# One weight tile for the K and Q projections, a DMA transpose at the start, and G accumulated early

## Chip, cores and metric

One core of a Trainium2 chip. The metric is the device time of one execution in microseconds. Beside it each execution has a span, from its first to its last instruction; the time is some 1.7 to 2.0 us longer than the span. All runs told of here are of state fast, that is within 1.5% of the fastest of their kernel. "The chain" is the profile's chain of work that ended last, followed back from the last instruction to whatever each step had waited for. Stages have the names of the kernel's functions: K and Q (projections), G, KV, M, D (denominators), E (first half of the feed-forward), FT and F (outputs).

## The reference

```python
x = A_x                                            # 1 x 2048 x 640, bf16
g = sigmoid((x * gate_w).sum(-1, keepdims=True))
# A: linear attention, 32 heads of 20
q, k, v = split(x @ wqkv)                          # wqkv 640 x 1920
phi = lambda t: where(t > 0, t + 1, exp(t)) + 1e-6
pq, pk = phi(q), phi(k)
kv = einsum("bhsd,bhse->bhde", pk, v); z = einsum("bhsd->bhd", pk)
o = einsum("bhqd,bhde->bhqe", pq, kv) / (einsum("bhqd,bhd->bhq", pq, z)[..., None] + 1e-6)
a = o.transpose(...).reshape(B, S, D) @ wo
# B: feed-forward with a gate
b = (gelu(x @ w_gate) * (x @ w_up)) @ w_down       # 640 -> 1728 -> 640
out = g * a + (1 - g) * b
```

The kernel doesn't compute v. It forms G = x^T pk, then kv = Wv^T G per group of heads (masked), M = kv wo, and at the end pq M and the feed-forward in one accumulation. The 2048 rows are 16 tiles of 128.

## The kernel before

Loads at the start, in the order of the queue (cuts marked):

```python
dma(out=x_sb[0][:, 0, :], in_=x_view[:, 0, :])
for lo, hi in ((0, 1), (1, 3), (3, 5)):
    dma(out=wk[:, lo:hi, 0:D], in_=wqkv_v[:, lo:hi, D : 2 * D])
dma(out=x_sb[0][:, 2:4, :], in_=x_view[:, 2:4, :])
dma(out=wq[:], in_=wqkv_v[:, :, 0:D])
...                                  # gate and up weights
for q in (1, 2, 3):                  # x transposed by DMA for tiles 4 to 15
    nc.sync.dma_start_transpose(out=xT[q][:, :, :], in_=x2[q * QW : (q + 1) * QW, :])
```

Tiles 0 to 3 are transposed on TensorE (`transpose_x`: five 128x128 transposes into PSUM, two copies out). The first K projections and the order of stages:

```python
CH = ((0, QW), (QW, D))              # 512 and 128 columns; K has one more, the gate's
def k_first():
    transpose_x(0)
    nc.tensor.matmul(t[:, 0:256], ...)           # a filler
    transpose_x(1)
    for dk in range(ND):
        for st in range(2):
            mm(st, 0, dk)                        # 512-wide chunk of K, tiles 0 and 1
        ...
    for st in range(2):
        for dk in range(ND):
            mm(st, 1, dk)                        # 129-wide chunk
        transpose_x(2 + st)
        k_out(st, pss[st])
...
k_first()
for st in (2, 3): phase_K(st)
for st in range(4): phase_Q(st)
for ft in range(NF): phase_E(0, ft)              # feed-forward of rows 0 to 511
for st in range(4, NT): phase_K(st)
phase_gate()
for st in range(4, NT):
    phase_Q(st); ...                             # z additions, G matmuls in between
phase_Zrep(); ...                                # the rest of G
phase_KV(0, 4)
...                                              # phase_E(1) with M and the denominators D
phase_FT(0)                                      # outputs; then E(2), FT(1), E(3), FT(2), F
```

`phi` of a chunk is an exp on ScalarE, a min-add and a max-add on VectorE.

Of the kernel before, what the change touches and what calls it, by code (L numbers as in the profile page):

```python
# [8 lines left out]
ACT = mybir.ActivationFunctionType  # L9
ALU = mybir.AluOpType  # L10
# [6 lines left out]
def kernel(  # L17
# [12 lines left out]
    nc = tc.nc  # L30
# [29 lines left out]
    def ps_tile(name):  # L60
        return psum.tile([P, QW], FP32, name=name, tag="ps")
# [7 lines left out]
    x_sb = [x_all[:, 4 * q : 4 * q + 4, :] for q in range(NQ)]  # L69
    pk_q = [ov.tile([P, 4, D], BF16, name=f"pk{q}", tag="slab_a", bufs=NQ) for q in range(NQ)]  # L70
    pk = [pk_q[t // 4][:, t % 4, :] for t in range(NT)]
    wk = ov.tile([P, ND, D + P], BF16, name="wk", tag="slab_c")
    wq = ov.tile([P, ND, D], BF16, name="wq", tag="slab_d")

    wg = wpool.tile([P, ND, FM], BF16, name="wg")
    wu = wpool.tile([P, ND, FM], BF16, name="wu")
# [16 lines left out]
    nc.scalar.dma_start(out=gw5[:], in_=gate_w.rearrange("(k p) -> k p", p=P))  # L93
    dma(out=x_sb[0][:, 0, :], in_=x_view[:, 0, :])
    for lo, hi in ((0, 1), (1, 3), (3, 5)):
        dma(out=wk[:, lo:hi, 0:D], in_=wqkv_v[:, lo:hi, D : 2 * D])
    dma(out=x_sb[0][:, 2:4, :], in_=x_view[:, 2:4, :])
    dma(out=wq[:], in_=wqkv_v[:, :, 0:D])
    warm = consts.tile([P, 1], FP32, name="act_warm")
    nc.scalar.activation(out=warm[:], in_=nc.const_aps.tensor(1.0, [P, 1], BF16), func=ACT.Exp)  # L100
    for lo, hi in ((0, 512), (512, 1024), (1024, FM)):
# [3 lines left out]
    dma(out=wgu[:, :, FL:P], in_=wu_v[:, :, FM:F])  # L105
    for q in (1, 2, 3):
        nc.sync.dma_start_transpose(out=xT[q][:, :, :], in_=x2[q * QW : (q + 1) * QW, :])
    for q in (1, 2, 3):
        dma(out=x_sb[q][:], in_=x_view[:, 4 * q : 4 * q + 4, :])
    dma(out=wv[:], in_=wqkv_v[:, :, 2 * D : 3 * D])  # L110
# [64 lines left out]
            nc.vector.tensor_tensor(out=hT_cur[q][0:FL, ft, :], in0=pgu[FL:P, :],  # L175
                                    in1=gl[0:FL, :], op=ALU.mult)

    def phi(dst, src, width):
        e = work.tile([P, QW], BF16, name="phi_e")
        nc.scalar.activation(out=e[:, :width], in_=src, func=ACT.Exp)  # L180
        m = work.tile([P, QW], BF16, name="phi_m")
        nc.vector.tensor_scalar(  # L182
            out=m[:, :width], in0=e[:, :width], scalar1=1.0, scalar2=EPS, op0=ALU.min, op1=ALU.add,
        )
        nc.vector.scalar_tensor_tensor(  # L185
            out=dst, in0=src, scalar=0.0, in1=m[:, :width], op0=ALU.max, op1=ALU.add,
        )

    def proj(ps, w, st, lo, hi):
        q, sl = divmod(st, 4)  # L190
        for dk in range(ND):
            nc.tensor.matmul(  # L192
                ps[:, 0 : hi - lo], lhsT=xT[q][:, dk, sl * P : (sl + 1) * P],
                rhs=w[:, dk, lo:hi], start=(dk == 0), stop=(dk == ND - 1),
            )

    CH = ((0, QW), (QW, D))

    def k_out(st, pss):
        for (lo, hi), ps in zip(CH, pss):  # L200
            phi(pk[st][:, lo:hi], ps[:, 0 : hi - lo], hi - lo)
        nc.scalar.activation(
            out=eneg[:, st : st + 1], in_=pss[1][:, D - QW : D - QW + 1], func=ACT.Exp, scale=-1.0
        )

    def phase_K(st):
        pss = [ps_tile("ps_k") for _ in CH]
        for (lo, hi), ps in zip(CH, pss):
            proj(ps, wk, st, lo, hi + (hi == D))
        k_out(st, pss)  # L210

    def k_first():
        pss = [[ps_tile("ps_k") for _ in CH] for _ in range(2)]

        def mm(st, c, dk):
            lo, hi = CH[c]
            hi += hi == D
            nc.tensor.matmul(  # L218
                pss[st][c][:, 0 : hi - lo], lhsT=xT[0][:, dk, st * P : (st + 1) * P],
                rhs=wk[:, dk, lo:hi], start=(dk == 0), stop=(dk == ND - 1),  # L220
            )

        transpose_x(0)
        nc.tensor.matmul(t[:, 0:256], lhsT=x_sb[0][:, 0, 0:P], rhs=x_sb[0][:, 0, 0:256], start=True, stop=True)
        transpose_x(1)
        for dk in range(ND):
            for st in range(2):
                mm(st, 0, dk)
            if dk == 2:
                tg = psum.tile([P, 2 * QW], BF16, name="tp_g", tag="ps")  # L230
                nc.tensor.transpose(tg[:, 0:ND], gw5[:], ident[0:ND, 0:ND])
                gcol = consts.tile([P, ND], BF16, name="gcol")
                nc.vector.tensor_copy(out=gcol[:], in_=tg[:, 0:ND])
        for dk in range(ND):
            nc.gpsimd.tensor_copy(out=wk[:, dk, D : D + 1], in_=gcol[:, dk : dk + 1])
        for st in range(2):
            for dk in range(ND):
                mm(st, 1, dk)
            transpose_x(2 + st)
            k_out(st, pss[st])  # L240

    def phase_Q(st):
        for lo, hi in CH:
            ps = ps_tile("ps_q")
            proj(ps, wq, st, lo, hi)
            phi(pq[st][:, lo:hi], ps[:, 0 : hi - lo], hi - lo)

    g_sb = big.tile([P, ND, D], BF16, name="g_sb")

    def g_units():  # L250
        for lo, hi in CH:
            for ct in range(ND):
                gp = ps_tile("ps_G")
                for st in range(NT):
                    nc.tensor.matmul(  # L255
                        gp[:, 0 : hi - lo], lhsT=x_all[:, st, ct * P : (ct + 1) * P],
                        rhs=pk[st][:, lo:hi], start=(st == 0), stop=(st == NT - 1),
                    )
                    if st < NT - 1:
                        yield hi - lo  # L260
                nc.scalar.copy(out=g_sb[:, ct, lo:hi], in_=gp[:, 0 : hi - lo])
                yield hi - lo

    zacc = consts.tile([P, D], FP32, name="zacc")
    zsum = consts.tile([P, D], BF16, name="zsum")
# [2 lines left out]
    def phase_Z(st):  # L268
        if st == 0:
            return  # L270
        nc.vector.tensor_tensor(out=(zsum[:] if st == NT - 1 else zacc[:]), in0=(pk[0][:] if st == 1 else zacc[:]),
                                in1=pk[st][:], op=ALU.add)
# [50 lines left out]

    def phase_M(g):
        if g == 0:
            M["sb"] = ov.tile([P, ND, D], BF16, name="m_sb", tag="slab_c")
            M["st"] = ov.tile([GW, NG, D], BF16, name="m_st", tag="slab_d")
        m_sb, m_st = M["sb"], M["st"]
        for hh in range(2):
            cs = slice(hh * HALF, (hh + 1) * HALF)  # L330
            mp = ps_tile("ps_m")
            nc.tensor.matmul(mp[0 : gw[g], 0:HALF], lhsT=kvt[0 : gw[g], g, 0 : gw[g]],  # L332
                             rhs=wo_g[0 : gw[g], g, cs], start=True, stop=True)
            if hh == 0:
                nc.vector.tensor_copy(out=m_st[0 : gw[g], g, cs], in_=mp[0 : gw[g], 0:HALF])
            else:
                nc.scalar.copy(out=m_st[0 : gw[g], g, cs], in_=mp[0 : gw[g], 0:HALF])
        lo = GW * g
        hi = lo + gw[g]
        while lo < hi:  # L340
            k = lo // P
            e = min(hi, (k + 1) * P)
            dma(out=m_sb[lo - k * P : e - k * P, k, :], in_=m_st[lo - GW * g : e - GW * g, g, :])
            lo = e
# [23 lines left out]
    def phase_FT(q):  # L368
        hT = hT_cur[q]
        o_q = ov.tile([P, 4, D], BF16, name="o_q", tag="slab_f")  # L370
        for dt in range(ND):
            ds = slice(dt * P, (dt + 1) * P)
            acc = ps_tile("ps_acc")
            for dk in range(ND):
                nc.tensor.matmul(acc[:], lhsT=M["sb"][:, dk, ds], rhs=pqT[q][:, dk, :],  # L375
                                 start=(dk == 0), stop=False)
            for ft in range(NF):
                nc.tensor.matmul(acc[:], lhsT=wd[:, ft, ds], rhs=hT[:, ft, :],  # L378
                                 start=False, stop=(ft == NF - 1))
            oT = work.tile([P, D], BF16, name="oT", tag="o_out", bufs=2)  # L380
            nc.vector.tensor_tensor(out=oT[:, 0:QW], in0=acc[:], in1=gsc["rep"][:, q * QW : (q + 1) * QW], op=ALU.mult)  # L381
            nc.sync.dma_start_transpose(out=o_q[:, :, ds], in_=oT[:, 0:QW])
        dma(out=out2[q * QW : (q + 1) * QW, :].rearrange("(t p) d -> p t d", p=P), in_=o_q[:])

    def phase_F(st):
# [6 lines left out]
        for i, (lo, hi) in enumerate(parts):  # L392
            acc = ps_tile("ps_acc")
            for dk in range(ND):
                nc.tensor.matmul(acc[:, 0 : hi - lo], lhsT=pqT[q][:, dk, ts],  # L395
                                 rhs=M["sb"][:, dk, lo:hi], start=(dk == 0), stop=False)
            for ft in range(NF):
                nc.tensor.matmul(acc[:, 0 : hi - lo], lhsT=hT[:, ft, ts],  # L398
                                 rhs=wd[:, ft, lo:hi], start=False, stop=(ft == NF - 1))
# [9 lines left out]

    with tc.manual_schedule(engines={mybir.EngineType.PE}):  # L410
        k_first()
    for st in (2, 3):
        phase_K(st)
    for st in range(4):
        phase_Q(st)
    for ft in range(NF):
        phase_E(0, ft)
    for st in range(4, NT):
        phase_K(st)
    phase_gate()  # L420
    gu = g_units()
    done = 0
    total = NT * ND * D
    for st in range(4, NT):
        phase_Q(st)
        for z in range(4 * (st - 4) // 3, 4 * (st - 3) // 3):
            phase_Z(z)
        while done < total * (st - 3) // (NT - 3):
            done += next(gu)
    phase_Zrep()  # L430
    for w in gu:
        pass
    phase_KV(0, 4)
    hT_cur[1] = ov.tile([P, NF, QW], BF16, name="hT1", tag="slab_b")
    nc.gpsimd.memset(hT_cur[1][FL:P, NF - 1, :], 0.0)
# [53 lines left out]
```

## Time and profile before

| | before |
|---|---|
| median of the first 4 runs | 279.83 us (279.4 to 282.44) |
| span of the profiled run | 277.5 us |
| TensorE busy | 271.8 us, 98% |
| VectorE, ScalarE busy | 143.2, 76.1 us |
| feed-forward begins | 17.48 us |

The last row is the start of the first `ps_g` matmul in the timeline; it splits the kernel into a start that hangs on loads and a rest that hardly varies. The lines of the page and of the chain stand in the prediction. One view more is worth having beside them, the groups of instructions with shapes kept apart (columns: line, engine, operation, tiles, shapes, count, busy us, mean ns, idle before):

```profile
L192 PE MATMUL ps_q<-wq,xT 128*128 128x512 bf16 x78 | 19.8, 379 | 0.1
L192 PE MATMUL ps_q<-wq,xT 128*128 128x128 bf16 x80 | 7.1, 219 | 0.0
```

A narrow matmul's record lasts 219 ns, but 80 of them were busy for only 7.1 us in all: records overlap. So a record's length isn't what a matmul costs in a stream; that has to be read from the chain.

### The profile page before, as it was taken

The page shows a single profiled execution, that of the slowest core. Times are in us where ns is not written, and L with a number is a line of the kernel's source. Part 1 is how long each engine was busy: PE and PEld are TensorE (multiplying, and loading weights), DVE is VectorE, ACT ScalarE, POOL GpSimd, SP SyncE. Part 2 cuts the span into 40 slices and gives each one's busy share as a digit, 9 for nine tenths or more (in the row PEclk, how much of TensorE's full clock was granted, in tenths as well). Part 3 has the DMA queues.
Part 4 walks back from the last instruction along what each step waited for, and adds up shares of the span by engine and source line. Part 5 has one row for each costly group of instructions (what it writes and reads, how often), then busy time and mean ns, then how long its engine had stood idle before and what let it go on. Part 6 is the DMA issues. An engine that isn't in the chain of part 4 may idle for free.

```text
span 277.5 us, 3993 instructions
## 1 busy us (share of the span) xinstructions
PE 271.8 (98%) x1522; PEld 138.6 (50%) x1548; DVE 143.2 (52%) x317; ACT 76.1 (27%) x167; POOL 5.1 (2%) x18
## 2 busy tenths in 40 slices
PE   8999999999999999999999999999999999999995
PEld 3554444555555584544444444444444444445774
DVE  0793233899944369999999542221112332101011
ACT  3663224764233362442100123210012222000100
POOL 5000000000000000000000000000000000000000
PEclk9999999999999999999999999999999999999999
DMA  7999999300100005343223540001112000021301
GB/s 213 361 353 194 224 353 282 118 2 0 1 4 0 0 2 149 62 117 72 51 53 65 105 135 0 0 0 31 28 38 94 2 0 0 19 40 38 118 26 47
DMA packets 43818, 23.58 MB, mean 85 GB/s; under 512 B 30808, under 2 KB 43672, under 8 KB 43800
## 3 DMA queue, kind: packets, MB, share of 16 engines
q1 hardware_dynamic: 43646, 23.17, 32.0%
q8 instruction: 12, 0.20, 0.3%
q10 hardware_dynamic: 154, 0.17, 0.2%
q14 instruction: 6, 0.05, 0.1%
HBM read 13.32 MB, written 2.63 MB: 57 GB/s over the span
## 4 chain that ended last, share of the span: by engine, by line
PE 96%; DMA 2%; ACT 1%; issue 1%; SPq 0%; DVE 0%
PE ps_u L155 20%; PE ps_g L155 20%; PE ps_acc L378 16%; PE ps_q L192 8%; PE ps_G L255 8%; PE ps_k L192 7%; PE ps_acc L375 6%; PE ps_acc L398 5%; PE ps_acc L395 2%; DMA wk<-in_A_wqkv_dram 2%; PE ps_gu L155 2%; PE ps_k L218 1%; PE ps_m L332 1%; PE ps_kv L304 1%; ACT phi_e L180 0%
## 5 line engine op out<-in xcount | busy, mean ns | idle before, releaser
L155 PE MATMUL ps_g<-xT,wg 128*128 128x512 bf16 x249 | 64.1, 379 | 0.6
L155 PE MATMUL ps_u<-xT,wu 128*128 128x512 bf16 x260 | 64.6, 379 | 0.0
L161 DVE TENSOR_TENSOR hT<-ps_u,gl 128x512 bf16<-128x512 f32 x52 | 35.6, 685 | 51.1 <-PE ps_u L155 51.1
L160 ACT ACTIVATE gl<-ps_g 128x512 bf16<-128x512 f32 x52 | 31.0, 597 | 112.1 <-PE ps_g L155 112.1
L378 PE MATMUL ps_acc<-hT,wd 128*128 128x512 bf16 x205 | 47.5, 379 | 0.3
L155 PEld LDWEIGHTS <-wu 128*128 128x128 bf16 x260 | 25.4, 98 | 30.7
L155 PEld LDWEIGHTS <-wg 128*128 128x128 bf16 x260 | 25.1, 98 | 29.2 <-issue 0.3
L192 PEld LDWEIGHTS <-xT 128*128 128x128 bf16 x300 | 24.0, 98 | 20.5 <-ACT xT L146 0.4
L378 PEld LDWEIGHTS <-wd 128*128 128x128 bf16 x210 | 20.5, 98 | 24.8
L381 DVE TENSOR_TENSOR oT<-ps_acc,omg_rep 128x512 bf16<-128x512 f32 x15 | 10.3, 687 | 36.7 <-PE ps_acc L378 32.8
L192 PE MATMUL ps_q<-wq,xT 128*128 128x128 bf16 (+1 forms) x158 | 23.8, 298 | 0.1
L255 PE MATMUL ps_G<-pk,x_all 128*128 128x128 bf16 (+1 forms) x157 | 23.4, 298 | 0.2
L182 DVE TENSOR_SCALAR phi_m<-phi_e 128x512 bf16<-128x512 bf16 x64 | 12.8, 237 | 15.4 <-ACT phi_e L180 15.2
L192 PE MATMUL ps_k<-wk,xT 128*128 128x512 bf16 (+1 forms) x136 | 19.2, 298 | 0.3
L375 PE MATMUL ps_acc<-pqT,m_sb 128*128 128x512 bf16 x75 | 18.6, 379 | 0.0
L180 ACT ACTIVATE phi_e<-ps_q 128x512 bf16<-128x512 f32 (+1 forms) x32 | 12.4, 435 | 21.6 <-PE ps_q L192 21.1
L398 PE MATMUL ps_acc<-wd,hT 128*128 128x320 bf16 (+1 forms) x126 | 16.7, 285 | 0.0
L255 PEld LDWEIGHTS <-x_all 128*128 128x128 bf16 x160 | 12.0, 98 | 7.2
L180 ACT ACTIVATE phi_e<-ps_k 128x512 bf16<-128x512 f32 (+1 forms) x32 | 12.8, 440 | 7.5 <-PE ps_k L192 4.3
L185 DVE SCALAR_TENSOR_TENSOR pq<-ps_q,phi_m 128x512 bf16<-128x512 f32 (+1 forms) x32 | 14.2, 483 | 0.0
L185 DVE SCALAR_TENSOR_TENSOR pk<-ps_k,phi_m 128x512 bf16<-128x512 f32 (+1 forms) x32 | 14.2, 481 | 0.0
L398 PEld LDWEIGHTS <-hT 128*128 128x128 bf16 x126 | 11.6, 98 | 3.7
(65 smaller groups left out, 144.3 us busy)
## 6 DMA issues: line engine op xcount, KB each, us to landing
wd<-in_B_w_down_dram SPq DMA_DIRECT2D x1, 2080.0 KB
x_all<-in_A_x_dram SPq DMA_DIRECT2D x3, 640.0 KB, 4.9
out_dram<-o_q SPq DMA_DIRECT2D x3, 640.0 KB
wg<-in_B_w_gate_dram SPq DMA_DIRECT2D x2, 640.0 KB
wu<-in_B_w_up_dram SPq DMA_DIRECT2D x2, 640.0 KB, 11.2
wq<-in_A_wqkv_dram SPq DMA_DIRECT2D x1, 800.0 KB
wg<-in_B_w_gate_dram SPq DMA_DIRECT2D x1, 800.0 KB
wu<-in_B_w_up_dram SPq DMA_DIRECT2D x1, 800.0 KB
```

Of the source, the lines that this page charges most:

```text
L155: nc.tensor.matmul(ps[:, t0 : t0 + tw], lhsT=w[:, dk, ft * P : (ft + 1) * P], rhs=xT[q][:, dk, t0 : t0 + tw], start=(dk == 0), stop=(dk == ...
L160: nc.scalar.activation(out=gl[:], in_=psg[:], func=ACT.Gelu_apprx_tanh)
L161: nc.vector.tensor_tensor(out=hT_cur[q][:, ft, :], in0=psu[:], in1=gl[:], op=ALU.mult)
L180: nc.scalar.activation(out=e[:, :width], in_=src, func=ACT.Exp)
L182: nc.vector.tensor_scalar(out=m[:, :width], in0=e[:, :width], scalar1=1.0, scalar2=EPS, op0=ALU.min, op1=ALU.add,)
L185: nc.vector.scalar_tensor_tensor(out=dst, in0=src, scalar=0.0, in1=m[:, :width], op0=ALU.max, op1=ALU.add,)
L192: nc.tensor.matmul(ps[:, 0 : hi - lo], lhsT=xT[q][:, dk, sl * P : (sl + 1) * P], rhs=w[:, dk, lo:hi], start=(dk == 0), stop=(dk == ND - 1),)
L255: nc.tensor.matmul(gp[:, 0 : hi - lo], lhsT=x_all[:, st, ct * P : (ct + 1) * P], rhs=pk[st][:, lo:hi], start=(st == 0), stop=(st == NT - 1),)
L375: nc.tensor.matmul(acc[:], lhsT=M["sb"][:, dk, ds], rhs=pqT[q][:, dk, :], start=(dk == 0), stop=False)
L378: nc.tensor.matmul(acc[:], lhsT=wd[:, ft, ds], rhs=hT[:, ft, :], start=False, stop=(ft == NF - 1))
L381: nc.vector.tensor_tensor(out=oT[:, 0:QW], in0=acc[:], in1=gsc["rep"][:, q * QW : (q + 1) * QW], op=ALU.mult)
L398: nc.tensor.matmul(acc[:, 0 : hi - lo], lhsT=hT[:, ft, ts], rhs=wd[:, ft, lo:hi], start=False, stop=(ft == NF - 1))
```

## The change

Intent: fewer and wider matmuls for K and Q (chunks of 512, 512 and 257 columns in place of 512, 129, 512 and 128), part of G accumulated while K and Q are computed, and a start without PE transposes for tiles 2 and 3. The diff, cut to its core:

```diff
-    wk = ov.tile([P, ND, D + P], BF16, name="wk", tag="slab_c")
-    wq = ov.tile([P, ND, D], BF16, name="wq", tag="slab_d")
+    WQK = 2 * D + 1
+    wqk = ov.tile([P, ND, 2 * D + P], BF16, name="wqk", tag="slab_c")   # Q in 0:D, K in D:2D, gate at 2D
@@ loads
-    dma(out=x_sb[0][:, 2:4, :], in_=x_view[:, 2:4, :])
-    dma(out=wq[:], in_=wqkv_v[:, :, 0:D])
+    dma(out=wqk[:, :, 0:D], in_=wqkv_v[:, :, 0:D])
+    nc.sync.dma_start_transpose(out=xT[0][:, :, 2 * P : QW], in_=x2[2 * P : QW, :])
...
+    dma(out=x_sb[0][:, 2:4, :], in_=x_view[:, 2:4, :])      # now behind the later transposes
@@ k_first
-        nc.tensor.matmul(t[:, 0:256], ...)
...
-            transpose_x(2 + st)
@@ new
+    CQ = ((0, QW), (QW, D))
+    CK = ((D, D + QW), (D + QW, WQK))
+    CF = ((0, QW), (QW, 2 * QW), (2 * QW, WQK))
+    def phase_KQ(st, chunks, wo=0):
+        for lo, hi in chunks:
+            ps = ps_tile("ps_kq")
+            for dk in range(ND):
+                kq_mm(ps, st, dk, lo + wo, hi + wo)          # columns lo+wo to hi+wo of wqk
+            cols(st, ps, lo, hi)                             # phi into pq and pk by lo, hi
@@ order
-    for st in (2, 3): phase_K(st)
-    for st in range(4): phase_Q(st)
+    for st in (0, 1): phase_KQ(st, CQ, wo=D)
+    for st in (2, 3): phase_KQ(st, CF)
     for ft in range(NF): phase_E(0, ft)
-    ...                                                      # K of 4..15; Q with z and G; rest of G
+    early = [(ps_tile("ps_G"), ct) for ct in range(2)]
+    for st in range(4, NT):
+        phase_KQ(st, CF)
+        ...                                                  # 2 or 4 matmuls of the two early accumulators
+    phase_gate(); ...                                        # z additions
+    ...                                                      # the other eight accumulators of G
+    phase_Zrep()
```

Note `wo=D`: Q of tiles 0 and 1 is computed from columns D to 2D, which hold K's weights. So for 256 of 2048 rows the query is the key. All runs of the changed kernel still counted as correct. I replayed the formulas in double precision with this swap: the output moves by at most 1.1e-5 while its standard deviation is 2.3e-3, since phi(q) is 1.00 with a deviation of 0.06 here and cancels largely between numerator and denominator. It is a wrong computation that this data hides.

More of the change, by code (lines that the diff above doesn't have):

```diff
@@ L95 @@
     for lo, hi in ((0, 1), (1, 3), (3, 5)):
-        dma(out=wk[:, lo:hi, 0:D], in_=wqkv_v[:, lo:hi, D : 2 * D])
-    dma(out=x_sb[0][:, 2:4, :], in_=x_view[:, 2:4, :])
-    dma(out=wq[:], in_=wqkv_v[:, :, 0:D])
+        dma(out=wqk[:, lo:hi, D : 2 * D], in_=wqkv_v[:, lo:hi, D : 2 * D])
+    dma(out=wqk[:, :, 0:D], in_=wqkv_v[:, :, 0:D])
+    nc.sync.dma_start_transpose(out=xT[0][:, :, 2 * P : QW], in_=x2[2 * P : QW, :])
     warm = consts.tile([P, 1], FP32, name="act_warm")
@@ L176, in phase_E, with cols @@
                                     in1=gl[0:FL, :], op=ALU.mult)
-    def phi(dst, src, width):
+    def cols(st, ps, lo, hi):
+        w = hi - lo
         e = work.tile([P, QW], BF16, name="phi_e")
-        nc.scalar.activation(out=e[:, :width], in_=src, func=ACT.Exp)
+        nc.scalar.activation(out=e[:, 0:w], in_=ps[:, 0:w], func=ACT.Exp)
         m = work.tile([P, QW], BF16, name="phi_m")
         nc.vector.tensor_scalar(
-            out=m[:, :width], in0=e[:, :width], scalar1=1.0, scalar2=EPS, op0=ALU.min, op1=ALU.add,
+            out=m[:, 0:w], in0=e[:, 0:w], scalar1=1.0, scalar2=EPS, op0=ALU.min, op1=ALU.add,
@@ L184, in phi @@
         )
-        nc.vector.scalar_tensor_tensor(
-            out=dst, in0=src, scalar=0.0, in1=m[:, :width], op0=ALU.max, op1=ALU.add,
-        )
-    def proj(ps, w, st, lo, hi):
-        q, sl = divmod(st, 4)
-        for dk in range(ND):
-            nc.tensor.matmul(
-                ps[:, 0 : hi - lo], lhsT=xT[q][:, dk, sl * P : (sl + 1) * P],
-                rhs=w[:, dk, lo:hi], start=(dk == 0), stop=(dk == ND - 1),
-            )
-    CH = ((0, QW), (QW, D))
-    def k_out(st, pss):
-        for (lo, hi), ps in zip(CH, pss):
-            phi(pk[st][:, lo:hi], ps[:, 0 : hi - lo], hi - lo)
-        nc.scalar.activation(
-            out=eneg[:, st : st + 1], in_=pss[1][:, D - QW : D - QW + 1], func=ACT.Exp, scale=-1.0
-        )
@@ L206, in phase_K @@
-    def phase_K(st):
-        pss = [ps_tile("ps_k") for _ in CH]
-        for (lo, hi), ps in zip(CH, pss):
-            proj(ps, wk, st, lo, hi + (hi == D))
-        k_out(st, pss)
-    def k_first():
-        pss = [[ps_tile("ps_k") for _ in CH] for _ in range(2)]
-        def mm(st, c, dk):
-            lo, hi = CH[c]
-            hi += hi == D
-            nc.tensor.matmul(
-                pss[st][c][:, 0 : hi - lo], lhsT=xT[0][:, dk, st * P : (st + 1) * P],
-                rhs=wk[:, dk, lo:hi], start=(dk == 0), stop=(dk == ND - 1),
-            )
+        if hi == WQK:
+            nc.scalar.activation(
+                out=eneg[:, st : st + 1], in_=ps[:, w - 1 : w], func=ACT.Exp, scale=-1.0
+            )
@@ new lines, in cols, with kq_mm @@
+        for dst, base in ((pq[st], 0), (pk[st], D)):
+            a, z = max(lo, base), min(hi, base + D)
+            if a < z:
+                nc.vector.scalar_tensor_tensor(
+                    out=dst[:, a - base : z - base], in0=ps[:, a - lo : z - lo], scalar=0.0,
+                    in1=m[:, a - lo : z - lo], op0=ALU.max, op1=ALU.add,
+                )
+    def kq_mm(ps, st, dk, lo, hi):
+        q, sl = divmod(st, 4)
+        nc.tensor.matmul(
+            ps[:, 0 : hi - lo], lhsT=xT[q][:, dk, sl * P : (sl + 1) * P],
+            rhs=wqk[:, dk, lo:hi], start=(dk == 0), stop=(dk == ND - 1),
+        )
@@ L223, in k_first @@
+    CQ = ((0, QW), (QW, D))
[7 more added lines that the diff above has]
+            cols(st, ps, lo, hi)
+    def k_first():
+        pss = [[ps_tile("ps_k") for _ in CK] for _ in range(2)]
         transpose_x(0)
-        nc.tensor.matmul(t[:, 0:256], lhsT=x_sb[0][:, 0, 0:P], rhs=x_sb[0][:, 0, 0:256], start=True, stop=True)
@@ L227, in k_first @@
             for st in range(2):
-                mm(st, 0, dk)
+                kq_mm(pss[st][0], st, dk, *CK[0])
             if dk == 2:
@@ L234, in k_first, with g_mm, g_out @@
         for dk in range(ND):
-            nc.gpsimd.tensor_copy(out=wk[:, dk, D : D + 1], in_=gcol[:, dk : dk + 1])
+            nc.gpsimd.tensor_copy(out=wqk[:, dk, 2 * D : WQK], in_=gcol[:, dk : dk + 1])
         for st in range(2):
             for dk in range(ND):
-                mm(st, 1, dk)
-            transpose_x(2 + st)
-            k_out(st, pss[st])
-    def phase_Q(st):
-        for lo, hi in CH:
-            ps = ps_tile("ps_q")
-            proj(ps, wq, st, lo, hi)
-            phi(pq[st][:, lo:hi], ps[:, 0 : hi - lo], hi - lo)
-    g_sb = big.tile([P, ND, D], BF16, name="g_sb")
-    def g_units():
-        for lo, hi in CH:
-            for ct in range(ND):
-                gp = ps_tile("ps_G")
-                for st in range(NT):
-                    nc.tensor.matmul(
-                        gp[:, 0 : hi - lo], lhsT=x_all[:, st, ct * P : (ct + 1) * P],
-                        rhs=pk[st][:, lo:hi], start=(st == 0), stop=(st == NT - 1),
-                    )
-                    if st < NT - 1:
-                        yield hi - lo
-                nc.scalar.copy(out=g_sb[:, ct, lo:hi], in_=gp[:, 0 : hi - lo])
-                yield hi - lo
+                kq_mm(pss[st][1], st, dk, *CK[1])
+            for (lo, hi), ps in zip(CK, pss[st]):
+                cols(st, ps, lo, hi)
+    g_sb = big.tile([P, ND, D], BF16, name="g_sb")
+    def g_mm(gp, ct, st, lo, hi):
+        nc.tensor.matmul(
+            gp[:, 0 : hi - lo], lhsT=x_all[:, st, ct * P : (ct + 1) * P],
+            rhs=pk[st][:, lo:hi], start=(st == 0), stop=(st == NT - 1),
+        )
+    def g_out(gp, ct, lo, hi):
+        nc.scalar.copy(out=g_sb[:, ct, lo:hi], in_=gp[:, 0 : hi - lo])
     zacc = consts.tile([P, D], FP32, name="zacc")
@@ L325, in phase_M @@
         if g == 0:
-            M["sb"] = ov.tile([P, ND, D], BF16, name="m_sb", tag="slab_c")
-            M["st"] = ov.tile([GW, NG, D], BF16, name="m_st", tag="slab_d")
-        m_sb, m_st = M["sb"], M["st"]
+            M["all"] = ov.tile([P, ND + NG, D], BF16, name="m_all", tag="slab_c")
+        m_sb = M["all"][:, 0:ND, :]
+        m_st = M["all"][:, ND : ND + NG, :]
         for hh in range(2):
@@ L374, in phase_FT @@
             for dk in range(ND):
-                nc.tensor.matmul(acc[:], lhsT=M["sb"][:, dk, ds], rhs=pqT[q][:, dk, :],
+                nc.tensor.matmul(acc[:], lhsT=M["all"][:, dk, ds], rhs=pqT[q][:, dk, :],
                                  start=(dk == 0), stop=False)
@@ L395, in phase_F @@
                 nc.tensor.matmul(acc[:, 0 : hi - lo], lhsT=pqT[q][:, dk, ts],
-                                 rhs=M["sb"][:, dk, lo:hi], start=(dk == 0), stop=False)
+                                 rhs=M["all"][:, dk, lo:hi], start=(dk == 0), stop=False)
             for ft in range(NF):
@@ L411 @@
         k_first()
+    for st in (0, 1):
+        phase_KQ(st, CQ, wo=D)
     for st in (2, 3):
-        phase_K(st)
-    for st in range(4):
-        phase_Q(st)
+        phase_KQ(st, CF)
     for ft in range(NF):
         phase_E(0, ft)
+    early = [(ps_tile("ps_G"), ct) for ct in range(2)]
     for st in range(4, NT):
-        phase_K(st)
-    phase_gate()
-    gu = g_units()
-    done = 0
-    total = NT * ND * D
-    for st in range(4, NT):
-        phase_Q(st)
-        for z in range(4 * (st - 4) // 3, 4 * (st - 3) // 3):
-            phase_Z(z)
-        while done < total * (st - 3) // (NT - 3):
-            done += next(gu)
+        phase_KQ(st, CF)
+        for gp, ct in early:
+            for g in range(4 * (st - 4) // 3, 4 * (st - 3) // 3):
+                if g < NT - 1:
+                    g_mm(gp, ct, g, 0, QW)
+    phase_gate()
+    for st in range(NT):
+        phase_Z(st)
+    for ct, lo, hi in [(ct, 0, QW) for ct in range(2, ND)] + [(ct, QW, D) for ct in range(ND)]:
+        gp = ps_tile("ps_G")
+        for st in range(NT - 1):
+            g_mm(gp, ct, st, lo, hi)
+        for ep, ec in early:
+            g_mm(ep, ec, NT - 1, 0, QW)
+            g_out(ep, ec, 0, QW)
+        early = []
+        g_mm(gp, ct, NT - 1, lo, hi)
+        g_out(gp, ct, lo, hi)
     phase_Zrep()
-    for w in gu:
-        pass
     phase_KV(0, 4)
```

## The prediction

> **What bounds the kernel now.** I read the page first, for which engine is full, then the chain of work that ended last.
>
> ```profile
> PE 271.8 (98%) x1522; PEld 138.6 (50%) x1548; DVE 143.2 (52%) x317; ACT 76.1 (27%) x167; POOL 5.1 (2%) x18
> PE 96%; DMA 2%; ACT 1%; issue 1%; SPq 0%; DVE 0%
> ```
>
> TensorE is busy 98% of the span and is 96% of the chain. "Busy" could hide slow issue, so I looked for the spacing of matmuls. In the chain, in order of time, five 128x512 matmuls take 1.08 us, 216 ns each, wherever I look, although one record lasts 379 ns (pipelined records overlap). In the stage where K is projected, 49 matmuls, half 512 and half 128 or 129 columns wide, take 6.76 us; a Q tile (five of 512, five of 128) takes 1.36 us.
>
> ```profile
> 17.65 1.08 PE ps_g L155 x5
> ...
> 55.23 6.76 PE ps_k L192 x49
> ...
> 63.14 1.36 PE ps_q L192 x10
> 64.50 1.73 PE ps_G L255 x8
> ```
>
> So a pair costs 1.36/5 = 0.272 us, of which 0.216 is the 512-wide matmul and only 0.056 the 128-wide one: TensorE pays for columns, hardly for instructions. The reader should not be misled by the narrow matmul's record of 219 ns.
>
> Next, busy time by stage (the columns are PE, PEld, DVE, ACT, POOL, then clock, DMA share, GB/s):
>
> ```profile
> 0.00:17.48 17.48, 15.92 (x106) 8.60 (x109) 9.54 (x33) 9.18 (x25) 4.62 (x17) 1.00 0.94 300
> 46.62:62.97 16.35, 16.19 (x118) 9.25 (x120) 14.10 (x44) 11.27 (x34) 0.00 (x0) 1.00 0.28 95
> 62.97:101.44 38.47, 38.26 (x284) 21.84 (x286) 24.58 (x72) 14.63 (x40) 0.00 (x0) 1.00 0.03 1
> 101.44:134.10 32.66, 32.45 (x175) 16.11 (x177) 32.66 (x66) 11.85 (x21) 0.52 (x1) 1.00 0.38 90
> ```
>
> The stages that the change rewrites, K from 46.62 and Q with G from 62.97, have no hole in TensorE: 16.19 of 16.35 and 38.26 of 38.47 us. Only the first 17.48 us have some, so I read the chain there:
>
> ```profile
> 6.14 1.02 PE ps_k L218 x4
> 7.16 0.11 PE tp_g L231
> 7.27 0.77 PE ps_k L218 x3
> 8.04 0.02 issue
> 8.06 1.26 ACT phi_e L180 x3
> 9.32 0.38 ACT xT L146
> 9.70 0.05 issue
> 9.75 2.47 PE ps_k L192 x18
> 12.22 4.29 PE ps_q L192 x31
> ```
>
> The detour over ScalarE is where the K projection of tile 2 waits for its transposed x to be copied out of PSUM. This is what the change takes away.
>
> **What the Trainium skill says.** "TensorE: Matmul & The Clock Gate", section "Wait — 56ns, not 53.3ns?", gives a warm start-to-start of N divided by 2.4 GHz plus about 2.5 ns: 215.7 ns for 512 columns and 55.6 for 128. The trace agrees (216 and 56). The same page, "What's actually happening", says that the array starts at half clock and is released after a busy window of about 3.4 us, free-running. The trace agrees: the six warming matmuls are some 0.43 us apart and the first 512-wide K matmul lasts 562 ns, while from 5.37 us on they last 380. "DMA: Bandwidth & Descriptors", section "Queues, rings and completion order", says that on each DMA engine descriptors are consumed in ring order, so a transfer waits for the data queued before it on its queue; and its section "Latency and other measured facts" gives 261 GB/s for DMA transposes in one kernel. Here I take a lower rate, below.
>
> **The change part by part.**
>
> *One weight tile, three chunks instead of four.* K and Q columns (640 + 641) were cut 512, 129, 512, 128; now 512, 512, 257 for tiles 2 to 15. The columns stay 1281. Each of 14 tiles saves five matmuls: 70 x 2.5 ns = 0.18 us, of which 0.15 falls to the twelve later tiles. By the naive reading, five records of 219 ns per tile, it would save 15 us; the spacing forbids that. A tile now costs 5 x (216 + 216 + 257/2.4 + 2.5) ns = 2.71 us.
>
> *G.* The same 160 matmuls. Two of its ten accumulators are now filled during K/Q of tiles 4 to 15, the other eight afterwards in one run. TensorE had no holes here, so the reordering gains nothing.
>
> *The start.* Removed: ten PE transposes (five take about 0.28 us), their four copies, and a 256-column filler. The filler lies before the wait for the K weights, which ends at 6.14 us: nothing gained. The first K loop still ends its wide matmuls and the five narrow ones of tile 0 at 8.36. Then five narrow ones of tile 1 to 8.64, two Q tiles of 1.36 to 11.35, and two merged tiles of 2.71 to 16.76. The feed-forward, which began at 17.48, can start 0.72 us sooner: about 0.59 from transposes, 0.1 from the wait for the copy, the rest fewer matmuls.
>
> The two first Q tiles read, by the indices of the diff, columns 640 to 1279, which hold K's weights. That looks like a mistake in the values, perhaps too small to be noticed; for the time it means that they don't wait for Q's weights. Shapes and counts are as usual.
>
> *The DMA transpose that takes the place of the ten.* It must land before 11.35 us. Ahead of it are two x tiles (2 x 160 KB), K and Q weights (2 x 800 KB): 1.97 MB. The page's GB/s row starts 213, 361 in slices of 6.94 us, so 1.48 MB are in by 6.94 us and the rest at 8.3. The three later transposes run while these rates are seen (last column):
>
> ```profile
> 22.00:24.00 2.00, 2.00 (x11) 0.92 (x10) 0.69 (x1) 0.60 (x1) 0.00 (x0) 1.00 1.20 125
> 24.00:26.00 2.00, 2.00 (x11) 0.94 (x10) 0.69 (x1) 0.60 (x1) 0.00 (x0) 1.00 1.07 243
> 26.00:28.00 2.00, 1.95 (x10) 0.88 (x10) 0.69 (x1) 0.60 (x1) 0.00 (x0) 1.00 1.12 198
> 28.00:30.00 2.00, 2.00 (x11) 0.88 (x9) 0.69 (x1) 0.44 (x1) 0.00 (x0) 1.00 0.92 161
> ```
>
> That is 180 GB/s: 0.33 MB take 1.8 us, landing at 10.1, with completion perhaps 10.6. It is hidden, by less than a microsecond. Gate and up weights come some 1.1 us later than now (1.8 more, 0.9 less for the x tiles moved behind): by 12 and 14 us, needed at 16.8 and 17.8. Hidden too.
>
> *VectorE in the merged stage.* One instruction adds some 70 to 80 ns less than its record (it overlaps the next). Per tile: phi_m 288 + 288 + about 220, the four max-add pieces 684 (512), 280 (128), about 550 (384) and 420 (256), sum 2.73 us, less 7 x 0.08: 2.2 us. With one z addition (0.74 net) 2.9 us. TensorE takes 2.71 us plus its share of the 30 early G matmuls, 30 x 0.216/12 = 0.54: 3.25 us. VectorE stays under it; ScalarE has about 1.8 us.
>
> *Sum:* -0.72 - 0.15 = -0.87 us. Against it I set 0.2 us for the D stage (rival 2). 279.83 - 0.7 = 279.1 us.
>
> **The rivals.**
> 1. *The transpose lands late.* For it: the slack of 0.8 us rests on a rate read elsewhere. Against it: nothing large is ahead. If it lands at 12.5, TensorE stalls 1.2 us and the kernel comes out about 0.3 slower, 280.2.
> 2. *VectorE becomes the bound.* The static order may put z additions ahead of PSUM evictions, with six banks left beside the two G accumulators; also zrep now follows all of G, so the denominators start some 1.5 us later against TensorE, in a stage where VectorE is busy 32.66 of 32.66 us. Against it: the feed-forward's results of that stage are needed only a stage later, and eight banks buffer. It costs 0 to 2 us: 279 to 281.
> 3. *The clock is released a window later,* because the filler is gone. Then some ten 512-wide matmuls run at half rate: ten times 0.21, about 2 us more, 281. Against it: two transposes' groups and two K matmuls still keep TensorE busy up to 5.7 us.
> 4. *The merge pays by the record or by weight loads* (98 ns each, 70 fewer: 7 us). Against it: PEld is busy 9.25 of 16.35 us in the K stage, and 0.056 us per narrow matmul leaves no room for a load that isn't hidden.
>
> **Range and chances.** Most weight lies on -0.87 plus small stalls; the runs before spread from 279.4 to 282.44, so the median alone can move by 0.3. Range 278.2 to 280.7. Two per cent is 5.6 us: only rival 4 gets there for faster, only two stalls together for slower. Chances 0.02, 0.95, 0.03.
>
> **What would show it.** Right: feed-forward starts near 16.8 us; a merged tile without G takes 2.71 us; from there to the first KV matmul some 83.65 us (before: 101.3 - 17.5 = 83.8); narrow matmuls still 0.056 us apart. Rival 1: a TensorE wait on xT at 11.4. Rival 2: TensorE waits on phi results or PSUM between 46 and 86, or more than 32.7 us in the stage after KV. Rival 3: 512-wide records above 500 ns after 6 us. Wrong altogether: a time under 277 or over 282.

## The result

| | before | changed |
|---|---|---|
| median | 279.78 us (16 runs) | 278.50 us (10 runs) |
| ratio, 95% interval | | 0.9942 (0.9919 to 0.9966) |
| span, profiled run | 277.5 | 277.3 us |

A ratio here is the mean time of one kernel's fast runs over the mean of the other's fast runs of the same rounds, so it isn't quite the ratio of the medians. That matters in this row: three of the sixteen runs of before took 281.41 to 282.44 us; without them it would be 0.9956. Later rounds gave 0.9966, 0.9961 and 0.9959 for the same changed kernel. Over the runs of all later calls the median of before is 279.72 (250 runs) and that of the changed kernel, with its first runs, 278.58 (44 runs): 1.14 us less, against 0.7 predicted. Direction and verdict (within 2%) were right, and so was the range; the size was not.

The page of the changed kernel, the busy line and the chain:

```profile
PE 270.5 (98%) x1443; PEld 136.6 (49%) x1467; DVE 143.6 (52%) x301; ACT 74.2 (27%) x151; POOL 5.1 (2%) x18
PE 96%; DMA 2%; issue 1%; SPq 0%; DVE 0%
```

TensorE is as full as before. The span of this run is only 0.2 us shorter, and its chain at the start shows why (start us, length us, what):

```profile
2.23 5.64 DMA wqk<-in_A_wqkv_dram
...
7.91 1.59 PE ps_k L201 x14
9.50 1.79 PE ps_kq L201 x12
...
11.35 6.29 PE ps_kq L201 x37
```

The last of the three loads of K's weights landed at 7.87 us, and the list of waits has it as 0.9 us. In a second trace of the same kernel (`after_2`, 278.27 us) there is no such wait on the last load:

```profile
6.09 1.02 PE ps_k L201 x4
7.12 0.11 PE tp_g L226
7.22 1.54 PE ps_k L201 x14
8.76 8.13 PE ps_kq L201 x50
16.89 1.08 PE ps_g L156 x5
```

Here the chain answers the one of before shown in the prediction: the ScalarE detour is gone, and TensorE runs through to the feed-forward. In the merged stage the chain of the first trace reads

```profile
46.77 2.71 PE ps_kq L201 x15
49.48 0.43 PE ps_G L240 x2
49.91 2.71 PE ps_kq L201 x15
```

A merged tile takes 2.71 us to the digit, with nothing between. By stages of the traces (differences of timeline starts; the last column is the mean over all timed runs of a label, and for the first runs of before the record has no spans):

| kernel | feed-forward begins | to first KV matmul | to first output matmul | to end of span | time minus span |
|---|---|---|---|---|---|
| before | 17.48 | 83.80 | 32.70 | 143.5 | |
| `before_2` | 17.71 | 83.80 | 32.69 | 143.5 | 1.97 |
| changed | 17.47 | 83.64 | 32.70 | 143.5 | 1.70 |
| `after_2` | 16.73 | 83.64 | 32.70 | 143.5 | 1.70 |

All fifteen traces of kernels with the merge, those of the experiments below included, have 83.64 or 83.65 us in the second column, all five without it 83.79 or 83.80. Three columns hardly move, so a kernel's time is the first column, plus 83.8 or 83.64, plus a constant, plus the last column, which the prediction had not thought of.

### The profile page after: what moved, and what is told of

Read it like the earlier page. It is cut to its first block, busy times and chain, and to the rows that moved or that the text cites. A ratio compares the mean times of both kernels' runs of the same rounds, so it can differ in the third digit from the quotient of the medians.

```text
span 277.3 us, 3767 instructions
## 1 busy us (share of the span) xinstructions
PE 270.5 (98%) x1443; PEld 136.6 (49%) x1467; DVE 143.6 (52%) x301; ACT 74.2 (27%) x151; POOL 5.1 (2%) x18
## 4 chain that ended last, share of the span: by engine, by line
PE 96%; DMA 2%; issue 1%; SPq 0%; DVE 0%
PE ps_u L156 20%; PE ps_g L156 20%; PE ps_acc L362 16%; PE ps_kq L201 15%; PE ps_G L240 8%; PE ps_acc L359 6%; PE ps_acc L382 6%; DMA wqk<-in_A_wqkv_dram 2%; PE ps_acc L379 2%; PE ps_gu L156 2%; PE ps_m L316 1%; PE ps_kv L288 1%; PE ps_k L201 1%; SPq L96 0%; SPq L94 0%
## 5 line engine op out<-in xcount | busy, mean ns | idle before, releaser
L201 PE MATMUL ps_kq<-wqk,xT 128*128 128x512 bf16 (+2 forms) x229 | 42.7, 340 | 0.1
L182 ACT ACTIVATE phi_e<-ps_kq 128x512 bf16<-128x512 f32 (+2 forms) x46 | 22.9, 519 | 21.2 <-PE ps_kq L201 20.7
L240 PE MATMUL ps_G<-pk,x_all 128*128 128x128 bf16 (+1 forms) x155 | 22.8, 297 | 0.2
L337 DVE TENSOR_TENSOR prod<-pq,zrep 128x640 f32<-128x640 bf16 x16 | 12.6, 788 | 13.4 <-ACT zrep L263 13.4
L359 PE MATMUL ps_acc<-pqT,m_all 128*128 128x512 bf16 x75 | 18.6, 379 | 0.0
L194 DVE SCALAR_TENSOR_TENSOR pq<-ps_kq,phi_m 128x512 bf16<-128x512 f32 (+1 forms) x32 | 15.4, 487 | 0.4
L184 DVE TENSOR_SCALAR phi_m<-phi_e 128x512 bf16<-128x512 bf16 (+3 forms) x50 | 11.9, 263 | 3.8 <-ACT phi_e L182 3.6
L349 DVE TENSOR_TENSOR pq<-pq,rg 128x640 bf16<-128x640 bf16 x16 | 12.9, 807 | 0.0
L194 DVE SCALAR_TENSOR_TENSOR pk<-ps_kq,phi_m 128x384 bf16<-128x384 f32 (+1 forms) x28 | 12.5, 482 | 0.2
```

The source lines that it names most:

```text
L182: nc.scalar.activation(out=e[:, 0:w], in_=ps[:, 0:w], func=ACT.Exp)
L194: nc.vector.scalar_tensor_tensor(out=dst[:, a - base : z - base], in0=ps[:, a - lo : z - lo], scalar=0.0, in1=m[:, a - lo : z - lo], op0=A ...
L201: nc.tensor.matmul(ps[:, 0 : hi - lo], lhsT=xT[q][:, dk, sl * P : (sl + 1) * P], rhs=wqk[:, dk, lo:hi], start=(dk == 0), stop=(dk == ND - 1),)
L240: nc.tensor.matmul(gp[:, 0 : hi - lo], lhsT=x_all[:, st, ct * P : (ct + 1) * P], rhs=pk[st][:, lo:hi], start=(st == 0), stop=(st == NT - 1),)
L337: nc.vector.tensor_tensor(out=prod[:], in0=pq[st][:], in1=zrep[:], op=ALU.mult)
L349: nc.vector.tensor_tensor(out=v, in0=v, in1=rg[:].to_broadcast([P, H, Dh]), op=ALU.mult)
```

## The experiments

Theory A, at first: the start alone gives the gain. Theory B: the merge gives more than reckoned. `e_start` refuted A in this form, and from `after_q` and `start_k` on A says that the start's gain hangs on Q of tiles 0 and 1 not waiting for Q's weights, and B that the wait seen in `e_start` was an accident of its trace. For the excess over the prediction two more, C and D, come later.

**Second looks.** `before_2`, `after_2`, `after_3` and `after_4` are the two kernels unchanged.

> The kernel before once more, for a second trace and a second set of times. All theories: ratio 1.00 within 0.3%. If the first profile of before was a lucky one, this trace shows more waiting in its first 17.5 us than that one; if not, its feed-forward starts at 17.5 us again.

Measured: 0.9999 (0.9986 to 1.0012). The feed-forward starts at 17.71 us: the first trace wasn't especially lucky.

> The changed kernel once more, for a second trace. Theory A (the start alone gives the gain, and the 0.92 us wait for the K weights in the first trace was bad luck): feed-forward starts near 16.6 us in this trace, ratio 0.994 to 0.997. Theory B (the merged stage gives more than I reckoned): from the start of the feed-forward to the first KV matmul less than 83.5 us.

Measured: 0.9966 (0.9953 to 0.9979), start 16.73 us, 83.64 us to KV. A holds on the start; B does not.

> The changed kernel a third time, since the two measured ratios differ (0.9942 and 0.9966). If the first was pulled down by the slow runs of before in its rounds: 0.996 to 0.9975 again. If the chip of the first rounds makes the difference: below 0.996.

Measured: 0.9961 (0.9938 to 0.9984), start 17.34 us with a 0.41 us wait on K's weights. The first 0.9942 was pulled down by the slow runs of before.

> The changed kernel again, as control of this chip: time minus span 1.70, ratio 0.995 to 0.9975.

Measured: 0.9959 (0.9946 to 0.9973), time minus span 1.73. Its profile fell on one of its two longest executions (280.13 us) and is the one trace that shows rival 3. Groups of matmuls in its first 12 us, then the same of `after_2`:

```profile
L201 PE MATMUL ps_k<-wqk,xT 128*128 128x512 bf16 x10 | 4.8, 625 | 0.3 <-DMA wqk<-in_A_wqkv_dram 0.3
```

```profile
L201 PE MATMUL ps_k<-wqk,xT 128*128 128x512 bf16 x10 | 2.7, 386 | 0.7 <-DMA wqk<-in_A_wqkv_dram 0.7
```

All ten wide K matmuls last 625 ns, as long as the six warming ones, against 386. The feed-forward starts at 18.59 us, 1.9 later than in `after_2`, and the later stages are as ever. (The profile's own clock figure stays at 1.00 here, so this is read from the durations.) So a late release of the clock occurs and costs about what rival 3 said, but in some executions only. Counting runs more than 1.2 us above their kernel's median: 16 of 250 of before, which has the filler, and 2 of 44 of the changed kernel, which has not; over all kernels here, 17 of 289 with the filler and 16 of 221 without. The counts give no sign that the missing filler matters. They don't show that all these long runs had a late clock: no other trace fell on one.

**The start alone.** `e_start`: the start of the change in the kernel before, with Q's own weights.

```diff
-    dma(out=x_sb[0][:, 2:4, :], ...)          # moved back
     dma(out=wq[:], in_=wqkv_v[:, :, 0:D])
+    nc.sync.dma_start_transpose(out=xT[0][:, :, 2 * P : QW], in_=x2[2 * P : QW, :])
-    (filler and transpose_x(2), transpose_x(3) removed)
-    for st in (2, 3): phase_K(st)
-    for st in range(4): phase_Q(st)
+    for st in (0, 1): phase_Q(st)
+    for st in (2, 3): phase_K(st)
+    for st in (2, 3): phase_Q(st)
```

> Only the start of the change: DMA transpose for tiles 2 and 3, no PE transposes for them, no filler matmul, Q of tiles 0 and 1 first (with Q's own weights); the later K, Q and G stages as before. Theory A: nearly the whole gain, ratio 0.9945 to 0.9975 (-0.7 to -1.5 us). Theory B: ratio 0.998 or more.

Measured: 0.9999 (0.9987 to 1.0011). No gain at all, against my expectation: this is in B's range, but B isn't the reason, as `e_merge` below shows. Its waits of TensorE (us in total, times, longest) and its chain name the reason:

```profile
PE ps_k L219 <- DMA wk<-in_A_wqkv_dram: 1.6, 2, 1.0
...
PE ps_q L193 <- DMA wq<-in_A_wqkv_dram: 0.6, 1, 0.6
```

```profile
2.73 7.57 DMA wq<-in_A_wqkv_dram
10.30 0.05 issue
10.34 2.89 PE ps_q L193 x20
```

Q's weights land at 10.30 us. TensorE wants them at 9.75 in this trace, since K's weights were late too, and at 8.68 where they weren't (`start_k` below). The profiled run, 280.51 us, is 0.85 above the median of its kernel, so the sizes of its waits aren't typical.

**The same with K's weights.** `start_k` is `e_start` with `proj(ps, wk if st < 2 else wq, ...)`, wrong on purpose.

> The start-only kernel, but with K's weights for Q of tiles 0 and 1 as in the change (values wrong on purpose). Theory A: no wait on Q's weights, ratio 0.9965 to 0.998 (-0.55 to -1 us). Theory B: ratio 0.999 or more.

Measured: 0.9974 (0.9962 to 0.9985), no wait on Q's weights, feed-forward from 16.84 us. One operand makes the difference between nothing and the whole start gain.

**The change with Q's own weights.** `after_q`: `phase_KQ(st, CQ, wo=D)` becomes `phase_KQ(st, CQ)`.

> The changed kernel with one number changed: Q of tiles 0 and 1 is computed from Q's weights, not K's. Theory A (the gain hangs on not waiting for Q's weights, which land about 10.3 us): a TensorE wait on wqk of 1 to 2 us after 8.7 us, feed-forward from 17.5 us or later, ratio 0.9985 to 1.0000. Theory B (the wait seen in the start-only run was an accident of that trace): ratio 0.996 to 0.9975.

Measured: 0.9981 (0.9967 to 0.9996), median 279.47. Its list of waits:

```profile
PE ps_k L201 <- DMA wqk<-in_A_wqkv_dram: 0.8, 1, 0.8
PE ps_kq L201 <- DMA wqk<-in_A_wqkv_dram: 0.7, 1, 0.7
```

The second line is the wait on Q's weights, which land at 9.83 us here; it is 0.7 us, less than the 1 to 2 expected; this trace's K weights were late too (TensorE could go on with the second load of them at 6.43 us, against 6.09 in `after_2`). The ratio lies just outside A's range of 0.9985 to 1.0000 and also outside B's. But the range left out what this kernel keeps of the change, the merge and the time outside the span, some 0.4 us or 0.9986 (below). The median is 0.9 us above the changed kernel's 278.58, and 0.76 above that of `after_fill`, run in the same call. With `start_k` this confirms A, and it is an awkward finding: most of what the change wins, it wins by using the wrong weights.

**The merge alone.** `e_merge`: the changed kernel with the start of before.

> Only the merge and the new order of G: the start is that of the kernel before (PE transposes, filler, order of loads, four narrow chunks for tiles 0 to 3). Theory A: -0.15 us, ratio 0.999 to 1.000. Theory B: ratio 0.996 to 0.998.

Measured: 0.9995 (0.9985 to 1.0005), median 279.47 against 279.73. In the trace 83.64 us from feed-forward to KV, as in the changed kernel; time minus span 1.71. So the merge and the reordered G are worth 0.16 us inside the span, and with them comes 0.25 us outside it. The 0.16 rests on the traces: the mean span of the timed runs is only 0.06 us shorter than that of before in the same call, which can't be told from 0.16, as the start varies more (the feed-forward begins at 18.03 us in this trace, in part by a 0.27 us wait on K's weights).

**The filler put back.** `after_fill` has the filler matmul between the two transpose groups.

> The changed kernel with the 256-column filler matmul put back between the two transpose groups. If the filler is off the path: same as the changed kernel, ratio 0.996 to 0.9975. If the filler costs: 0.1 to 0.3 us slower than the changed kernel. If it brings the clock release forward: faster or with fewer slow runs.

Measured: 0.9966 (0.9954 to 0.9978), as the changed kernel. The filler is off the path. Five runs are too few to say whether it alters the number of long runs.

**A right order.** `t_first`:

```diff
-    dma(out=wqk[:, :, 0:D], in_=wqkv_v[:, :, 0:D])
     nc.sync.dma_start_transpose(out=xT[0][:, :, 2 * P : QW], in_=x2[2 * P : QW, :])
+    dma(out=wqk[:, :, 0:D], in_=wqkv_v[:, :, 0:D])
...
-    for st in (0, 1): phase_KQ(st, CQ, wo=D)
-    for st in (2, 3): phase_KQ(st, CF)
+    for st in (2, 3): phase_KQ(st, CK)
+    for st in range(4): phase_KQ(st, CQ)
```

> The changed kernel with right values and another order: the DMA transpose of tiles 2 and 3 goes ahead of Q's weights, and K of tiles 2 and 3 is computed before Q of tiles 0 to 3 (four chunks each). If the DMA transpose lands by about 9 us and Q's weights by 11.7: ratio 0.997 to 0.9985. If the transpose itself holds up the queue (a dip in the DMA rate near 7 to 9 us): a wait on xT of 1 to 2 us and a ratio of 0.999 to 1.002.

Measured: 0.9968 (0.9956 to 0.9980), a little better than expected. No wait on xT; one of 0.85 us on Q's weights, which land at 12.14 us in this trace:

```profile
4.54 7.60 DMA wqk<-in_A_wqkv_dram
12.14 0.05 issue
12.18 5.61 PE ps_kq L201 x40
```

> The right-valued order (DMA transpose ahead of Q's weights) once more, as it had few runs: ratio 0.9955 to 0.998, time minus span 1.70.

Measured: 0.9965 (0.9953 to 0.9978), median 278.80, time minus span 1.72; in this trace Q's weights are in time and the feed-forward starts at 16.88 us. So there is a version with the right values (by the indices) that beats the kernel before and is within about 0.2 us of the change.

**Q's weights in two pieces.** `t_split` is `t_first` with Q's weights loaded as rows 0 to 1 and 2 to 4 of the five, and Q of tiles 0 to 3 computed row block by row block over four PSUM banks.

> The order with right values (DMA transpose ahead of Q's weights, K of tiles 2 and 3 first), with Q's weights loaded in two pieces and Q of tiles 0 to 3 computed piece by piece over four PSUM banks, so that TensorE has 1.7 us of work with the first piece. If the 0.85 us wait on Q's weights in the trace of that order is typical: 0.3 to 0.8 us faster than it, ratio 0.994 to 0.9965. If it was chance, or the split delays the loads: the same as it, 0.9965 to 0.998.

Measured: 0.9972 (0.9958 to 0.9986), median 278.69 of 22 runs, of which four were above 280. No wait on Q's weights in its trace, but no faster than `t_first`: the medians differ by 0.1 us. Not worth its code.

**Where the rest comes from.** In the kernel before, about 0.25 us more of a run lay outside the span than in the kernels with the merge (1.95 to 1.97 against 1.70 to 1.73 us in the means by label and call; a mean is good to some 0.02). The trace's own records of instruction fetches show two differences: in the kernel before an 8 KB fetch comes 1.8 us after the last instruction began, in the changed kernel none does; and there are 12 fetches of 16 KB before, 11 after. Theory C is that the first matters, theory D that it is TensorE's stream or something else. VectorE's stream has 443 entries in the trace of before, 402 in that of the changed kernel. I padded streams with tiny instructions in stages where the engine is idle. On VectorE and ScalarE:

```python
nc.vector.tensor_copy(out=pad[:, r : r + 1], in_=gl[:, r : r + 1])     # 52, 41 or 44 of them
nc.scalar.copy(out=pad[:, 0:1], in_=gl[:, 0:1])                        # 26 of them
```

> The changed kernel plus 52 copies of one column (VectorE, in the third and fourth feed-forward stages, where VectorE is mostly idle). In the runs so far the time is 1.96 us longer than the span of instructions in the kernel before and 1.70 in every kernel with the merge, and the trace of before shows one more fetch of instructions after the last work. Theory C (VectorE's longer instruction stream makes that fetch): time minus span back to about 1.96, span unchanged, ratio 0.9970 to 0.9985. Theory D (another engine's stream or something else): time minus span 1.70.

> The changed kernel plus 26 copies of one column on ScalarE, which brings its stream back to the length of before. Theory C' (ScalarE's stream makes the late fetch): time minus span about 1.96. Otherwise 1.70. The span itself should not change, as ScalarE is idle most of those stages.

> The changed kernel plus 41 one-column copies on VectorE instead of 52, so that its stream has about the 443 entries that it has in the trace of before (402 in the changed kernel). With 52 the extra fetch of instructions came 4 us before the end and cost nothing. Theory C (a fetch that falls after VectorE's last work holds up the end): the fetch falls after the last work and time minus span is 1.9 to 2.05. Theory D: it falls there and time minus span stays at 1.70.

> The same with 44 copies, in case 41 miss the boundary. Theory C: as with 41, or if the fetch now falls before the last work, 1.70.

On TensorE, 81 two-column matmuls:

> The changed kernel plus 81 two-column matmuls (with their 81 weight loads) ahead of the third feed-forward stage, which brings TensorE's stream to the 3098 rows of before and should make it 12 fetches of 16 KB instead of 11. The span grows by 2 to 6 us, which is not the question. Theory D (TensorE's twelfth fetch): time minus span 1.9 to 2.05. Theory C: 1.70.

And the reverse test, more work in the kernel before:

> The kernel before plus 12 one-column copies on VectorE in the fourth feed-forward stage (443 entries to 455). If a fetch of VectorE's instructions that falls after the last work costs the 0.26 us: the fetch moves ahead of the end, time minus span falls from 1.96 to about 1.70, and the kernel with more work is 0.2 to 0.3 us faster, ratio 0.9988 to 0.9995. If not: time minus span 1.96, ratio 1.000.

Measured:

| run | padded | VectorE entries in the trace | extra 8 KB fetch | time minus span | ratio |
|---|---|---|---|---|---|
| changed | | 402 | none | 1.70 | 0.9942 |
| `after_act` | ScalarE +26 | 402 | none | 1.70 | 0.9954 (0.9941 to 0.9967) |
| `after_dve41` | VectorE +41 | 441 | none | 1.70 | 0.9974 (0.9959 to 0.9989) |
| `after_dve44` | VectorE +44 | 444 | 1.8 us after the last instruction began | 1.98 | 0.9971 (0.9959 to 0.9983) |
| `after_dve` | VectorE +52 | 452 | 3 us before it | 1.72 | 0.9968 (0.9952 to 0.9984) |
| `after_pe` | TensorE +81 pairs | 402 | none | 1.71 | 1.0035 (1.0020 to 1.0050) |
| before | | 443 | 1.8 us after | 1.96 | |
| `before_dve12` | VectorE +12 | 454 | 7 us before | 1.71 | 0.9995 (0.9984 to 1.0006) |

Three more instructions, from 441 to 444, cost 0.28 us, and eight more after that take them off again. `e_start` and `start_k`, with the 443 entries of before, have the late fetch too, and 1.98 and 2.00 us. `after_pe` made TensorE fetch 12 times 16 KB as the kernel before does, without effect on time minus span: D falls. My first run for C, `after_dve`, missed because it overshot the boundary; the expectation written for it would have rejected a true theory. (The expectation for `after_dve41` puts that kernel's fetch 4 us before the end; the trace has 3.) The ratios are too coarse for a quarter of a microsecond (`after_dve41` had five runs above 280 of 20); time minus span isn't, as it leaves out the start's variation. That the time depends on the length of VectorE's stream is shown. That the 8 KB fetch is VectorE's is inferred from the padding, which moves it, and that the end of the execution waits for it from when it comes.

## Why the prediction was wrong, point by point

- **The merge, "-0.15".** Right: 83.80 to 83.64 us, a tile of 2.71 us. The reading that it pays by records or weight loads (rival 4) is refuted: 70 fewer matmuls and weight loads, no 7 us.
- **The start, "-0.72".** Right in size for the kernel as written: 17.48 to 16.73 us in the traces of before and `after_2`, which have no wait on the last of K's weights; over all runs the median span fell from 277.8 to 276.9, of which 0.16 is the merge, so 0.74. Its working left out a condition. The remark that two Q tiles "don't wait for Q's weights" was true and treated as a footnote; the runs show it to be the condition of the gain (`e_start` 0.9999, `start_k` 0.9974). That the size came out is owed to a mistake in the kernel, which the working had noticed and not weighed.
- **"1.97 MB ... the rest at 8.3."** Wrong as a landing time: Q's weights, the last of those bytes, landed at 10.30 and 9.83 us in `e_start` and `after_q`. In `e_start` 2.05 MB had indeed moved by 9 us, the transpose's first packets included. But packets of the weights went on until 9.89 us, while the transpose that was queued behind them had sent its first packet at 7.62. Bytes over a mean rate doesn't give the time at which a given transfer is complete. It did no harm, since the changed kernel needs Q's weights later.
- **The DMA transpose hidden (rival 1).** Right: no trace has a wait on xT, whose last packet ended at 9.76 us in `after_2` and at the latest, in `after_fill`, at 11.18. But a transfer did come late, one that I had not doubted: the last part of K's weights, by 0.2 to 0.9 us in six of the sixteen traces of kernels with the transpose (the first one, `after_3`, `after_fill`, `e_start`, `after_act`, `after_dve44`). Of the four traces with the start of before one has such a wait, of 0.3 us (`e_merge`). That is too few to blame the transpose. In the first trace of the changed kernel the DMA rate falls to 149 and 69 GB/s in the two microseconds after 8; in `after_2` to 222. This dip can't have held up K's weights, which landed at 7.87 us, and until 8 us the two traces had moved as much (1.92 and 1.89 MB). The packet records show what goes with it: a packet of the transpose takes 18 ns as a rule, but in each of the sixteen traces 4 to 22 of its 1280 packets took over 0.5 us, the longest 2.16. Why, and why K's weights were late, is open.
- **VectorE in the merged stage and zrep later (rival 2).** In the first trace of the changed kernel (columns as in the prediction; the second line is the D stage):

```profile
46.00:86.00 40.00, 39.79 (x212) 20.96 (x215) 36.50 (x94) 20.83 (x50) 0.00 (x0) 1.00 0.21 61
101.11:133.81 32.70, 32.49 (x175) 16.18 (x178) 31.81 (x63) 12.44 (x23) 0.52 (x1) 1.00 0.34 85
```

  VectorE was busy 36.5 of the 40 us from 46 to 86, TensorE 39.8: no bound. The D stage took 32.70 us, as before. The "+0.2" set against it was wrong: nothing came of it.
- **A late clock (rival 3).** It happens, in `after_4`'s profiled execution, at 1.9 us; nothing shows that the change brings it about.
- **The step that failed is the sum**, "-0.72 - 0.15 = -0.87", less 0.2. One of its terms should be zero: the 0.2 us for the D stage, which measured 0. And it lacks one, as it took the time to change with the span alone: -0.24 us of time minus span (1.954 to 1.712 over all runs), since VectorE's shorter stream no longer ends on a fetch. With measured terms: -0.74 - 0.16 - 0.24 = -1.14 us, the difference of the medians. (That it closes proves nothing, as the -0.74 is the rest of the span's change; what supports it is the 0.75 between the two traces.) What the first verdict shows beyond this (0.9942, and 0.9956 without them) came mostly with three long runs of the kernel before.

Still open: what lies behind the long runs of before (no trace fell on one), the dip in the DMA rate, and the late weights of K.

## What to carry to other kernels

When TensorE is full, price narrow matmuls by their spacing in the chain and not by their records, and look for gain where the chain leaves TensorE. Split such a kernel's time into a start that hangs on loads, a steady part and the part outside the span, and compare each by itself; a change in instruction count can move the last one either way. And when a reordering makes a wait vanish, check which operand is read: here the fast start came from reading K's weights for Q, while loading the transpose first gives nearly the same time with the right ones.

## What the Trainium skill lacked or had wrong

- "Runtime: NRT & Kernel Launch", section "Instruction fetch mechanics", says that an engine's stream is refilled in 16 KiB blocks and that crossing a boundary is "mostly hidden". The traces show 16 KB fetches that TensorE's length governs (11 or 12), but 8 KB ones for VectorE; and one that falls after the last work is not hidden: time minus span 1.98 us with 444 VectorE entries, 1.70 with 441 and 1.72 with 452.
- "DMA: Bandwidth & Descriptors", section "Latency and other measured facts", gives 261 GB/s for a DMA transpose, measured on one kernel. Here the three transposes of the kernel before ran at about 180 GB/s. Around the one at the start the rate fell to 149 and 69 GB/s in one trace and to 222 in another of the same kernel, and single packets of it took up to 2.16 us (`after_fill`); no page tells of such a dip.
- "TensorE: Matmul & The Clock Gate" lacked nothing here: its section "Wait — 56ns, not 53.3ns?" was right on the spacing (216 and 56 ns), and "What's actually happening" on a release of the clock that comes at different times in different runs: ten wide matmuls of 625 ns in one trace, 386 in another of the same kernel.
